# A fused retention and gated-MLP kernel: paired blocks from unit 8, DMA transposes from unit 10, and loads held until the transposes before them have landed

## Chip, cores, metric

One core of one Trainium2 chip. The metric is the device time of one execution in microseconds (us). A "ratio" is the mean time of one kernel's fast runs over the mean of the other kernel's fast runs of the same rounds on the same chip, so it is not quite the ratio of the medians that stand beside it.

The engines: PE is TensorE (matmul), ACT is ScalarE, DVE is VectorE, POOL is GpSimd, SP is SyncE. Here POOL only issues loads (after the first two us), and SP issues the transposes by DMA and the output stores.

## The reference

```python
def _attn_ref(q, k, v):                      # q, k, v: 8 batches, 8 heads, 576 rows, 64 wide, float32
    scores = (1.0 / np.sqrt(D_)) * np.matmul(q, k.transpose(0, 1, 3, 2))
    gamma = 1.0 - 2.0 ** (-5.0 - np.arange(H))
    Dmat = np.where(rel >= 0, gamma[:, None, None] ** rel[None, :, :], 0.0)   # rel = row - column
    return np.matmul(scores * Dmat[None], v)

def _moe_ref(x, w_in, w_out):                # x: 4608 x 512, w_in: 512 x 2048, w_out: 2048 x 512
    h = x @ w_in
    g = h * (1.0 / (1.0 + np.exp(-1.702 * h)))
    return g @ w_out
# x is the attention output with the heads side by side
```

## The kernel before

The 4608 rows are cut into 36 units of 128 rows (all 8 heads of a unit together). A unit needs k and q with rows on the partitions (as loaded, bf16) and also transposed (`qkT`). Per unit PE computes scores (k against q, inside the unit), inter (q against the running state of earlier units), values (masked scores against scaled V) and state (the update of k times V). Four units make a chunk of 512 columns for the MLP, whose long matmuls (`up`, `down`) fill the rest of PE's time. The attention work of later units is slotted between the long matmuls of earlier chunks.

Units 0 to 11 are handled one by one: PE transposes k and q (`head_in`), DVE copies the result out of PSUM, then scores, values, state. From unit 12 on, units go in pairs (`block`), and k and q are transposed by DMA.

```python
NLD, NVN, NQT = 12, 10, 10        # buffers for k/q, V, transposed k/q
osb = [sb(f"osb{i}", [P, DM], FP32) for i in range(4)]      # output row blocks

def transpose_pe(u, bank, eng):             # used by head_in
    ...
    for j in range(2 * HP):                 # eight 128x128 transposes on PE
        op("pe", lambda e, j=j: e.matmul(t[:, j, :], kq[sl][...], ident.ap(), is_transpose=True), ...)
    ...                                     # then one copy PSUM -> qkT
def transpose_dma(u):
    op("sp", lambda e: e.dma_start_transpose(qkT[u % NQT].ap(), kq[sl]...), ...)

def down(c, i, ybanks):                     # four of 16 matmuls of one output row block
    ...
    if s < 3: return
    o = u % 4
    op("act", lambda e: e.activation(osb[o].ap(), y, AF.Copy), reads=[bank], writes=[f"osb{o}"])
    ...                                     # then the store, issued by SP

def fetch(m, after=()):                     # loads of pair m, issued by POOL
    for u in (2 * m, 2 * m + 1):
        if u < NU:
            load_kq(u, after)               # a key in `after` holds the loads until it is written
            load_v(u)
def block(m, done=False):
    a, b = 2 * m, 2 * m + 1
    ...                                     # inter, values of a, b; scores of a + 2, b + 2
    fetch(m + 4)
    ready_t(m + 3)                          # two DMA transposes
    ready_v(m + 2)                          # DVE scales two V

play(16, lambda i: down(0, i, ("H0", "H1")), {
    1: [lambda: head_mid(9)],
    3: [lambda: head_in(10, "dve"), lambda: head_out(9)],
    5: [lambda: head_mid(10)],
    7: [lambda: head_in(11, "dve"), lambda: head_out(10), lambda: ready_t(7), lambda: fetch(8, ...)],
    9: [lambda: head_mid(11), lambda: ready_v(6)],
    11: [lambda: head_out(11)],
})
# for each m: block(m), then eight up (U) and eight down (D) steps, interleaved
```

Each engine runs its own program in order. A helper tracks every buffer's writer and readers and inserts the waits, so a load never overwrites a buffer in use.

## Time and profile before

| | before |
|---|---|
| median of 3 runs | 312.8 us (312.46 to 312.85) |
| span of the profiled run | 311.0 us, clock 1.0 |

The list of waits of PE in before (who waited for whom: us in total, times, longest):

```profile
PE psS L325 <- DMA kq<-in_k_dram: 1.3, 2, 0.7
PE psH L507 <- DVE zero L243: 1.2, 1, 1.2
PE psS L414 <- ACT qkT L330: 0.9, 2, 0.5
PE psS L325 <- DVE kq L623: 0.7, 1, 0.7
PE psO L433 <- DVE pm_1 L423: 0.5, 2, 0.3
PE psH L325 <- DMA kq<-in_q_dram: 0.4, 1, 0.4
```

Nearly all of these 5.0 us lie in the first 20 us (`psS L325` and its like are the first transposes).

The view of the transposed tile in before, its last line (from issue of a DMA to its landing, over the 24 transposes):

```profile
DMA to landing us min/median/max: 3.1/11.1/15.0
```

A transpose by DMA can land in 3.1 us, but most of them share the engines with loads and take about three times that or more (9.1 to 15.0 us). Since PE does not wait, this costs nothing.

The timeline of PE in before (start us, length us, what; a matmul's length includes its latency, so read the spacing of starts):

```profile
51.06 0.61 PE L311 MATMUL psS<-ident,kq 128*128 128x128 bf16 x8
51.51 1.91 PE L471 MATMUL psH<-xT,w_in_sb 128*128 128x256 bf16 x16
53.35 0.40 PE L414 MATMUL psS<-qkT 64*128 64x128 bf16 x8
53.68 1.92 PE L471 MATMUL psH<-xT,w_in_sb 128*128 128x256 bf16 x16
...
76.02 0.62 PE L414 MATMUL psS<-qkT 64*128 64x128 bf16 x16
76.58 1.90 PE L454 MATMUL psH<-xT,w_in_sb 128*128 128x512 bf16 x8
...
89.98 0.39 PE L395 MATMUL psO<-qkT,kv_2 128*128 128x128 bf16 x4
```

Eight transposes of a unit hold PE for 0.45 us (51.06 to 51.51), scores of one unit 0.33 us (53.35 to 53.68), scores of two units together 0.56 us (76.02 to 76.58). The last line is the first work of the block of units 12 and 13, the place where both kernels have done the same PE work except for what the change removes.

### The profile page before, as it was taken

The page shows a single profiled execution, that of the slowest core. Times are in us where ns is not written, and L with a number is a line of the kernel's source. Part 1 is how long each engine was busy: PE and PEld are TensorE (multiplying, and loading weights), DVE is VectorE, ACT ScalarE, POOL GpSimd, SP SyncE. Part 2 cuts the span into 40 slices and gives each one's busy share as a digit, 9 for nine tenths or more (in the row PEclk, how much of TensorE's full clock was granted, in tenths as well). Part 3 has the DMA queues.
Part 4 walks back from the last instruction along what each step waited for, and adds up shares of the span by engine and source line. Part 5 has one row for each costly group of instructions (what it writes and reads, how often), then busy time and mean ns, then how long its engine had stood idle before and what let it go on. Part 6 is the DMA issues. An engine that isn't in the chain of part 4 may idle for free.

```text
span 311.0 us, 5149 instructions
## 1 busy us (share of the span) xinstructions
PE 301.9 (97%) x2169; PEld 155.7 (50%) x2169; DVE 134.5 (43%) x272; ACT 123.4 (40%) x225; POOL 105.6 (34%) x132
## 2 busy tenths in 40 slices
PE   6799999999999999999999999999999999999994
PEld 2444588655454545454545454545454545444441
DVE  5761984597445542545363625362627150100000
ACT  9666345301433333333333333333343434343411
POOL 9999923015699935334454300000000000000000
PEclk9999999999999999999999999999999999999999
DMA  9999999999999999999999999923210102010012
GB/s 150 184 207 188 190 203 175 176 187 157 182 118 200 168 163 150 170 135 176 179 141 190 145 148 182 142 47 86 45 68 2 67 2 67 2 67 34 36 67 67
DMA packets 113752, 39.40 MB, mean 127 GB/s; under 512 B 102785, under 2 KB 106881, under 8 KB 113729
## 3 DMA queue, kind: packets, MB, share of 16 engines
q0 software_dynamic: 80016, 22.55, 74.7%
q1 hardware_dynamic: 33712, 16.52, 30.9%
q8 instruction: 17, 0.28, 0.4%
q14 instruction: 7, 0.05, 0.1%
HBM read 36.70 MB, written 9.44 MB: 148 GB/s over the span
## 4 chain that ended last, share of the span: by engine, by line
PE 92%; POOL 3%; DMA 2%; DVE 2%; ACT 0%; issue 0%; POOLq 0%
PE psH L454 36%; PE psS L485 33%; PE psH L471 5%; PE psH L485 5%; PE psO L433 3%; PE psS L414 3%; DMA vn<-in_v_dram 2%; PE psS L347 2%; PE psO L485 2%; POOL kq L203 2%; PE psO L395 1%; PE psS L311 1%; POOL vn L217 1%; DVE vp L302 0%; DVE xT L443 0%; DVE pm_0 L423 0%
## 5 line engine op out<-in xcount | busy, mean ns | idle before, releaser
L454 PE MATMUL psH<-xT,w_in_sb 128*128 128x512 bf16 x512 | 127.3, 380 | 0.0
L459 ACT ACTIVATE gT<-psH 128x512 bf16<-128x512 f32 x128 | 76.4, 597 | 116.1 <-PE psH L454 116.1
L485 PE MATMUL psS<-w_out_sb,gT 128*128 128x512 bf16 x480 | 117.3, 379 | 0.0
L454 PEld LDWEIGHTS psH<-xT,w_in_sb 128*128 128x128 bf16 x512 | 47.8, 98 | 58.7 <-ACT gT L459 3.2
L485 PEld LDWEIGHTS psS<-w_out_sb,gT 128*128 128x128 bf16 x480 | 46.0, 98 | 51.7
L203 POOL DMA_DIRECT2D kq<-in_k_dram x39 | 35.6, 921 | 43.3 <-DMA qkT<-kq 22.7
L203 POOL DMA_DIRECT2D kq<-in_q_dram x39 | 35.5, 919 | 15.2 <-issue 15.2
L217 POOL DMA_DIRECT2D vn<-in_v_dram x39 | 36.0, 932 | 9.3 <-issue 5.0
L423 DVE TENSOR_TENSOR pm_0<-psS,mask 128x512 bf16<-128x512 f32 x32 | 22.0, 687 | 37.6 <-PE psS L414 37.5
L493 ACT ACTIVATE osb<-psS 128x512 f32<-128x512 f32 x30 | 17.9, 597 | 30.4 <-PE psS L485 30.4
L443 DVE TENSOR_TENSOR xT<-psO,gq 128x512 bf16<-128x512 f32 x36 | 23.5, 682 | 11.4 <-PE psO L433 11.4
L302 DVE TENSOR_TENSOR vp<-vn,vfac 128x512 bf16<-128x512 f32 x36 | 23.7, 685 | 2.6 <-DMA vn<-in_v_dram 2.5
L423 DVE TENSOR_TENSOR pm_1<-psS,mask 128x512 bf16<-128x512 f32 x32 | 21.8, 680 | 0.0
L377 DVE TENSOR_TENSOR kvf<-psS,kvf 64x256 f32<-64x256 f32 x24 | 10.1, 421 | 26.2 <-PE psS L347 26.0
L471 PE MATMUL psH<-xT,w_in_sb 128*128 128x256 bf16 x128 | 15.2, 273 | 0.0
L485 PE MATMUL psH<-w_out_sb,gT 128*128 128x512 bf16 x64 | 15.0, 380 | 0.0
L476 ACT ACTIVATE gT<-psH 128x512 bf16<-128x512 f32 x16 | 9.6, 597 | 11.5 <-PE psH L471 11.5
L414 PE MATMUL psS<-qkT 64*128 64x128 bf16 x288 | 12.2, 218 | 1.1 <-ACT qkT L330 0.9
L433 PE MATMUL psO<-pm_0,vp 128*64 128x128 bf16 x144 | 13.1, 224 | 0.0
L433 PE MATMUL psO<-pm_1,vp 128*64 128x128 bf16 x144 | 12.5, 223 | 0.5 <-DVE pm_1 L423 0.5
L471 PEld LDWEIGHTS psH<-xT,w_in_sb 128*128 128x128 bf16 x128 | 12.0, 98 | 1.9 <-issue 0.2
L375 DVE COPY kvf<-psS 64x256 f32<-64x256 f32 x12 | 5.0, 420 | 18.2 <-PE psS L347 18.1
(78 smaller groups left out, 171.9 us busy)
## 6 DMA issues: line engine op xcount, KB each, us to landing
out_dram<-osb SPq DMA_DIRECT2D x32, 256.0 KB, 3.1
vn<-in_v_dram POOLq DMA_DIRECT2D x31, 256.0 KB, 20.0
kq<-in_k_dram POOLq DMA_DIRECT2D x31, 128.0 KB, 21.4
kq<-in_q_dram POOLq DMA_DIRECT2D x31, 128.0 KB, 21.3
w_in_sb<-in_moe_w_in_dram POOLq DMA_DIRECT2D x4, 512.0 KB, 11.2
w_out_sb<-in_moe_w_out_dram POOLq DMA_DIRECT2D x4, 512.0 KB, 19.6
vn<-in_v_dram POOLq DMA_DIRECT2D x8, 128.0 KB, 23.1
out_dram<-osb SPq DMA_DIRECT2D x8, 128.0 KB, 4.3
```

Of the source, the lines that this page charges most:

```text
L203: e.dma_start(kq[sl][p0 : p0 + n, i, :].rearrange("p (h d) -> p h d", d=DH), src[b, :, s0 : s0 + n, :].rearrange("h p d -> p h d"),)
L217: e.dma_start(vn[sl][p0 : p0 + n, :, :], v[b, :, s0 : s0 + n, :].rearrange("h p d -> p h d"),)
L302: op("dve", lambda e: e.tensor_tensor(vp[u % NVP].ap(), vn[sl].ap(), vfac[:, ty, :, None].to_broadcast([P, H, DH]), ALU.mult), reads=[f"vn ...
L414: op("pe", lambda e, hp=hp, hh=hh, bank=bank: e.matmul(by_pair(bank)[:, hp, :], qt[64 * hh : 64 * hh + 64, hp, :], qt[64 * hh : 64 * hh + ...
L423: op("dve", lambda e: e.tensor_tensor(pm[u % 4][hh].ap(), by_pair(bank), m[:, None, :].to_broadcast([P, HP, P]), ALU.mult), reads=[bank, " ...
L433: op("pe", lambda e, hp=hp, hh=hh: e.matmul(ob[64 * hh : 64 * hh + 64, hp, :], vp[u % NVP][:, 2 * hp + hh, :], pm[u % 4][hh][:, hp, :], st ...
L443: op("dve", lambda e: e.tensor_tensor(xT[ch % 3][:, :, 128 * j : 128 * j + 128], by_pair(bank), gq[:, ty, :, :], ALU.mult), reads=[bank] + ...
L454: op("pe", lambda e, a=a: e.matmul(hb, w_in_sb[:, a, P * f : P * f + P], xT[c % 3][:, a, :], start=(a == 0), stop=(a == HP - 1)), reads=[f ...
L459: op("act", lambda e: e.activation(gT[c % 2][:, f, :], hb, AF.Gelu_apprx_sigmoid), reads=[bank], writes=[f"gT{c % 2}_{f}"])
L471: op("pe", lambda e, a=a, f=f, j=j: e.matmul(hb[:, j, :], w_in_sb[:, a, P * f : P * f + P], xT[c % 3][:, a, n], start=(a == 0), stop=(a == ...
L485: op("pe", lambda e, f=f: e.matmul(y, gT[c % 2][:, f, P * r : P * r + P], w_out_sb[:, f, :], start=(f == 0), stop=(f == NF - 1)), reads=[f ...
L493: op("act", lambda e: e.activation(osb[o].ap(), y, AF.Copy), reads=[bank], writes=[f"osb{o}"])
```

## The change

Its intent: take the transposes of units 10 and 11 off PE, handle units 8 to 11 in pairs, and keep DMA transposes quick by letting no load run beside them. The core of the diff:

```diff
-        def fetch(m, after=()):
+        def fetch(m, held=None):
+            after = () if held is None else [f"qkT{held % NQT}q"]
             for u in (2 * m, 2 * m + 1):
                 if u < NU:
-                    load_kq(u, after)
-                    load_v(u)
+                    load_v(u, "pool", after)
+            for u in (2 * m, 2 * m + 1):
+                if u < NU:
+                    load_kq(u)
@@ block
-            fetch(m + 4)
-            ready_t(m + 3)
-            ready_v(m + 2)
+            if m > 4:
+                ready_t(m + 3)
+                fetch(m + 4, 2 * m + 7)
+                ready_v(m + 2)
@@ loads of the start: k, q of 8 and 9, then V of 8 to 11, then k, q of 10 and 11
-            load_v(u)
-        for u in (10, 11):
-            load_kq(u)
+        load_kq(8)
+        load_kq(9)
...
+        for u in range(8, 12):
             load_v(u)
+        load_kq(10)
+        load_kq(11)
@@ schedule
-        fetch(6)
+        ready_t(5)
+        fetch(6, 11)
+        ready_t(6)
...
+            6: [lambda: ready_v(4), lambda: scores_of(4)],
         play(16, lambda i: down(0, i, ("H0", "H1")), {
-            ... (units 9, 10, 11 one by one, with PE transposes)
+            1: [lambda: state(9)],
+            5: [lambda: ready_v(5)],
+            6: [lambda: block(4)],
+            9: [lambda: state(10), lambda: fetch(7, 13)],
+            11: [lambda: state(11)],
+            12: [lambda: ready_v(6)],
+            14: [lambda: ready_t(7), lambda: fetch(8, 15)],
         })
...
-            for x in "UUDDUDUDUDUDDDUU" if m == 5 else "DDUDUDUDUDUDDUUU":
+            for x in "DDDDBDDUDDUUUUUUU" if m == 5 else "DDUDUDUDUDUDDUUU":
+                if x == "B":
+                    block(m)
+                    continue
```

`fetch(6, 11)` means: the loads of units 12 and 13 (pair 6) wait until the transpose of unit 11 has landed. POOL issues in order, so all six loads of the pair wait. The kernel before already held the loads of pairs 7 and 8 in this way (for the transposes of 13 and 15), with k and q ahead of V; new are the hold of pair 6, the holds from pair 9 on, and V first.

## The prediction

> **What bounds the kernel now.** TensorE (PE). The page gives PE busy 301.9 of 311.0 us (97%); PE has 92% of the chain that ended last. The list of waits shows 5.0 us of PE waits, all on set-up and first loads. After 20 us PE never idles, although the DMA row stands at 9 tenths until about 200 us. Loads are hidden: a transpose by DMA lands 3.1 us after issue when nothing else is queued (201 us) but 9 to 15 us among loads (86 to 187 us), still in time. That agrees with the Trainium skill, "DMA: Bandwidth & Descriptors", "Issuing engines are not separate DMA queues": all queues share 16 engines. So quicker transposes buy nothing by themselves; only PE work counts.
>
> **What changes on PE** (timeline, issue spacing):
> - Transposes of units 10 and 11 leave PE; a block of eight takes 0.45 us (51.06 to 51.51): -0.9 us. (Their 0.69 us DVE copies are off the path.)
> - Paired scores of 8/9 and 10/11: 16 matmuls take 0.56 us against 2 x 0.33: -0.2 us. Paired values: 0.57 against 2 x 0.35: -0.25 us.
> - Fewer insertions between the long matmul groups: about -0.2 us.
> Sum about -1.5 us. Before 51 us and after unit 12's block the PE program is the same.
>
> **What it adds: a serial chain of load pair, transposes, next pair.** k/q of unit 11 should land at about 60.3 us, transposes 10 and 11 at about 62.5 and 63.5; the new pair block asks for them at about 63.5: no wait or a few tenths. Loads of 12/13 now start at about 64 (before: 38 to 52). One link, measured on the existing held fetch: first issue 68.8, last load landing 77.9, second transpose 80.2, next issue 80.6: 11.9 us; V first makes it about 12.8. So transposes 13, 15, 17 land at about 76, 89, 102, asked for at about 77, 90, 105. PE's period is 15.7 us per pair, so the chain gains on PE and no later stall is expected.
> The tight place: SyncE issues in order, so the first output stores wait behind the transposes of 12/13 (about 74.4). Row block 4 needs the output buffer of row block 0 before ScalarE can free bank S2, which unit 13's scores want at about 77.3. Stores land 2.4 to 4.5 us after issue, 77 to 79: a PE stall of about 0.7 us (0 to 2).
>
> **Prediction.** 312.8 - 1.5 + 0.7 = 312.0 us; 8 in 10 between 310.6 and 313.6. Faster by over 2%: 1%; within 2%: 97%; slower by over 2%: 2%.
>
> **What would show it.** PE's transposes in blocks of eight fall from 64 to 48, DMA transposes rise from 24 to 26, landing in 3 to 5 us (median 11.1 before), with no gain from that. Before 51 us the timelines agree. The block of unit 12 (inter against kv_2, 89.98 us before) starts about 89.2; from there on both take the same time. A PE wait under 2 us appears at the scores of 12/13 or 10/11, released by ScalarE's osb copy or a transpose.
>
> **What would make it wrong.** A chain link over 14.5 us (stores and transposes slowing loads): then 14/15 come late at 90 us and output buffers run out later, costing 2 to 5 us. Or no stall at all: 311.3. Or DVE, blocked in order on V of the next pair, delaying masks.

## More of the kernel before

Lines of the page of before (busy time, then two rows in 40 equal slices of the span, each digit the busy share in tenths, one DMA queue, and the shares of the chain that ended last):

```profile
span 311.0 us, 5149 instructions
...
PE 301.9 (97%) x2169; PEld 155.7 (50%) x2169; DVE 134.5 (43%) x272; ACT 123.4 (40%) x225; POOL 105.6 (34%) x132
...
PE   6799999999999999999999999999999999999994
...
DMA  9999999999999999999999999923210102010012
...
q8 instruction: 17, 0.28, 0.4%
...
PE 92%; POOL 3%; DMA 2%; DVE 2%; ACT 0%; issue 0%; POOLq 0%
```

PE is busy 97% of the span and nearly the whole chain. The DMA row is full until about 200 us.

## The result, and the profile after

| | before | after |
|---|---|---|
| median of 6 runs | 312.9 us (312.46 to 313.25) | 312.75 us (311.35 to 313.32) |
| ratio of fast runs | 1 | 0.9989 (95%: 0.9967 to 1.0011) |
| span of the profiled run | 311.0 us | 311.1 us |
| the same in a later set of five rounds | 312.85 us (312.56 to 312.99) | 313.65 us (311.94 to 314.86) |
| ratio there | 1 | 1.0026 (0.9998 to 1.0054) |

The two kernels are the same within noise, but the new one scatters: over 3.5 us in twelve runs, where before stays within 0.8 us in either set. Three of the twelve runs, and the median of the later set (313.65), lie above the upper end of the predicted range (313.6).

The page of after, the lines that answer to those of before:

```profile
span 311.1 us, 5121 instructions
...
PE 300.9 (97%) x2153; PEld 155.3 (50%) x2153; DVE 133.3 (43%) x270; ACT 123.5 (40%) x225; POOL 105.9 (34%) x132
...
PE   7789999999899999999999999999999999999994
...
DMA  9999999979989899896999989699910102010012
...
PE 70%; POOL 15%; DMA 14%; issue 1%; ACT 0%; SPq 0%; POOLq 0%
```

PE lost 1 us of busy time, and the 8 in the eleventh slice of its row (78 to 86 us) is new: PE waits there. The chain that ended last is now PE for 70% only; loads (POOL, DMA) make up the rest.

The list of waits of PE in after:

```profile
PE psS L325 <- DMA kq<-in_k_dram: 1.4, 2, 0.8
PE psH L507 <- DVE zero L243: 1.2, 1, 1.2
PE psS L414 <- ACT qkT L330: 1.1, 3, 0.5
PE psS L414 <- ACT osb L493: 1.0, 1, 1.0
PE psO L433 <- DVE pm_1 L423: 0.6, 2, 0.3
PE psH L325 <- DMA kq<-in_q_dram: 0.4, 1, 0.4
PE psS L414 <- DMA qkT<-kq: 0.2, 1, 0.2
```

Two lines are new: 1.0 us for the output copy (`ACT osb`) and 0.2 us for a transpose. The view of the transposed tile in after, last line:

```profile
DMA to landing us min/median/max: 3.0/3.1/4.8
```

The transposes are more than three times quicker, as intended. Timeline of after around the largest wait (SP, ACT, POOL and PE; in brackets the idle time before and what ended it):

```profile
72.17 3.54 SPq L338 DMA_TRANSPOSE qkT<-kq  x2
...
75.77 1.55 SPq L499 DMA_DIRECT2D out_dram<-osb  x3
...
77.45 0.40 PE L414 MATMUL psS<-qkT 64*128 64x128 bf16 x8
...
78.22 0.60 ACT L493 ACTIVATE osb<-psS 128x512 f32<-128x512 f32 x1 [3.96 <-DMA out_dram<-osb]
78.27 1.78 POOL L217 DMA_DIRECT2D vn<-in_v_dram  x2 [8.23 <-DMA qkT<-kq]
...
78.87 0.40 PE L414 MATMUL psS<-qkT 64*128 64x128 bf16 x8 [1.02 <-ACT osb L493]
```

Read it in order. SP issues the transposes of 12 and 13 when their k and q have landed, until 75.71 us. Only then do the stores of the first output row blocks go out (75.77), though those blocks had been ready for up to 14 us (ACT had copied the first at 61.5). ACT wants to write row block 4 into the same buffer as row block 0 and waits for that store to land (3.96 us, until 78.22). Its copy frees PSUM bank S2, which the second eight scores (unit 13) need. PE waits 1.0 us.

The two smaller places, timeline of PE in after:

```profile
63.58 0.94 PE L414 MATMUL psS<-qkT 64*128 64x128 bf16 x16
...
89.72 0.39 PE L395 MATMUL psO<-qkT,kv_2 128*128 128x128 bf16 x4
90.04 0.40 PE L414 MATMUL psS<-qkT 64*128 64x128 bf16 x8
90.59 0.40 PE L414 MATMUL psS<-qkT 64*128 64x128 bf16 x8 [0.15 <-DMA qkT<-kq]
```

The sixteen scores of 10 and 11 take 0.94 us instead of 0.62, because the transpose of 11 landed at 64.07 us. The second eight scores at 90.59 waited for the transpose of 15, which landed at 90.54.

How much is that? In an undisturbed block the second eight matmuls start 0.055 us after the last of the first eight. Measured against that, the three blocks lost 0.31, 1.18 and 0.31 us: 1.80 us. At the first matmul behind the block of units 12/13 before stands at 91.42 us and after at 91.49. So PE work and switches saved 0.07 less than the waits cost: 1.73 us saved, 1.80 us given back. From there to the end both take 219.6 us (311.03 - 91.42, 311.09 - 91.49).

### The profile page after: what moved, and what is told of

The parts are those of the page before. It is cut to its first block, busy times and chain, and to the rows that moved or that the text cites. A ratio compares the mean times of both kernels' runs of the same rounds, so it can differ in the third digit from the quotient of the medians.

```text
span 311.1 us, 5121 instructions
## 1 busy us (share of the span) xinstructions
PE 300.9 (97%) x2153; PEld 155.3 (50%) x2153; DVE 133.3 (43%) x270; ACT 123.5 (40%) x225; POOL 105.9 (34%) x132
## 4 chain that ended last, share of the span: by engine, by line
PE 70%; POOL 15%; DMA 14%; issue 1%; ACT 0%; SPq 0%; POOLq 0%
PE psS L485 31%; PE psH L454 30%; DMA kq<-in_q_dram 11%; POOL kq L203 8%; POOL vn L217 4%; DMA qkT<-kq 3%; PE psO L485 2%; PE psO L433 2%; PE psS L414 2%; PE psS L347 1%; PE psO L395 1%; POOL w_out_sb L232 1%; POOL w_in_sb L226 1%; PE psO L402 0%; ACT osb L493 0%
## 5 line engine op out<-in xcount | busy, mean ns | idle before, releaser
L217 POOL DMA_DIRECT2D vn<-in_v_dram x39 | 34.3, 919 | 111.3 <-DMA qkT<-kq 111.3
L433 PE MATMUL psO<-pm_1,vp 128*64 128x128 bf16 x144 | 12.2, 223 | 0.6 <-DVE pm_1 L423 0.6
L433 PE MATMUL psO<-pm_0,vp 128*64 128x128 bf16 x144 | 12.7, 223 | 0.0
L347 PE MATMUL psS<-vp,kq 128*128 128x128 bf16 x128 | 12.4, 219 | 0.0
```

The costliest lines, as they stand in the source:

```text
L217: e.dma_start(vn[sl][p0 : p0 + n, :, :], v[b, :, s0 : s0 + n, :].rearrange("h p d -> p h d"),)
L433: op("pe", lambda e, hp=hp, hh=hh: e.matmul(ob[64 * hh : 64 * hh + 64, hp, :], vp[u % NVP][:, 2 * hp + hh, :], pm[u % 4][hh][:, hp, :], st ...
```

## The experiments

Twelve kernels ran, all correct, each with five rounds. Four groups shared a chip and the runs of before: e1, e2, e4, e7; then e5, e6, e10, e11; then e9, e12, e13; then e14 alone. In the profiles of the experiments 36 matmul records are missing (2117 instead of 2153; 34 in e14), which shows as waits of 0.16 us for "issue" at regular places; they are left out below.

| run | what | median us (range) | ratio to before (95%) |
|---|---|---|---|
| e1_osb8 | eight output buffers | 316.14 (315.26 to 316.59) | 1.0093 (1.0079 to 1.0106) |
| e2_kqfirst | k, q of 10, 11 before their V | 311.82 (311.10 to 312.99) | 0.9961 (0.9945 to 0.9976) |
| e4_pairs_pe | pairs, but PE transposes, no first hold | 311.91 (311.67 to 312.48) | 0.9965 (0.9953 to 0.9977) |
| e7_f6 | no hold for units 12, 13 | 318.78 (318.19 to 319.27) | 1.0181 (1.0168 to 1.0194) |
| e5_hold_before | before, with hold and V first | 312.77 (312.63 to 313.02) | 1.0002 (0.9990 to 1.0014) |
| e6_both | e1 and e2 together | 312.05 (310.78 to 315.21) | 0.9996 (0.9954 to 1.0038) |
| e10_hold_first | hold for the first transpose of a pair | 311.32 (311.05 to 311.49) | 0.9953 (0.9940 to 0.9965) |
| e11_best | e2 and e10 together | 311.03 (310.76 to 311.29) | 0.9946 (0.9934 to 0.9958) |
| e9_hold_early | no hold from pair 9 on | 315.11 (313.77 to 317.37) | 1.0079 (1.0046 to 1.0112) |
| e12_hf_osb8 | e1 and e10 together | 311.03 (310.92 to 311.21) | 0.9945 (0.9932 to 0.9957) |
| e13_after_again | after, unchanged | 313.65 (311.94 to 314.86) | 1.0026 (0.9998 to 1.0054) |
| e14_osb8_shift | e1 with PE's instruction fetches moved | 312.46 (312.11 to 312.79) | 0.9985 (0.9973 to 0.9998) |

### Part alone: the loading order and the hold, in before

```diff
 # before
-                    load_kq(u, after)
-                    load_v(u)
+                    load_v(u, "pool", after)     # V of both units, then k and q of both
...
-            fetch(m + 4)
-            ready_t(m + 3)
+            ready_t(m + 3)
+            fetch(m + 4, [f"qkT{(2 * m + 7) % NQT}q"])
```

> The kernel before with only the loading part of the change in its steady loop: V of a pair ahead of its k and q, and from pair 9 on the next pair's loads held until the last transpose of the pair before. No pairing, units 10 and 11 still transposed on PE. Theory: transposes land in 3 to 5 us instead of 9 to 15 us, and the time does not move (ratio 0.998 to 1.002), since PE had no wait there. Rival (quicker transposes or a less loaded DMA speed something up): ratio below 0.997.

Measured: ratio 1.0002. The view of the transposed tile in this run, last line:

```profile
DMA to landing us min/median/max: 3.0/3.2/4.9
```

The median fell from 11.1 to 3.2 us and the time did not move. A wait that nobody has on the critical path is worth nothing, however long it looks.

### Part alone: pairing, with the transposes on PE

```diff
 # after
-        ready_t(5)
-        fetch(6, 11)
+        fetch(6)
@@ play(16, down ...)
+            2: [lambda: head_in(10, "dve", "S2")],
+            4: [lambda: head_in(11, "dve", "S0")],
```

> Pairing alone: the kernel after, but units 10 and 11 are transposed on PE (in two single blocks between the long matmuls) and the loads of 12 and 13 are not held. PE does 16 transposes more than after (+0.9 us) but the chain starts early, so no wait at the scores of 11, 13 and 15 (-1.7 us). Main theory: about 0.7 us faster than before, ratio about 0.997 to 0.998; the profile shows no PE wait after 20 us. Rival (pairing saves nothing, insertions are free): ratio 1.000 or above.

Measured: 0.9965, and no wait of PE after 38 us. The rival falls: pairs and fewer insertions are real time. The saving (0.35% of 312.9 us, 1.1 us) was more than the 0.65 us that the prediction's terms for them add up to, and this kernel, which still does two units' transposes on PE, was faster than the full change in either set of that (0.9989 and 1.0026; the interval of the first overlaps by a little).

### Undo one hold: the loads of units 12 and 13

```diff
-        fetch(6, 11)
+        fetch(6)
```

> The kernel after, with the hold removed from the loads of units 12 and 13 alone. Theory: the hold there protects the transposes of 10 and 11; without it they share the 16 DMA engines with the loads and land 2 to 4 us later than 62.3 and 64.1 us, so PE waits 2 to 4 us at the scores of 10/11, while the waits at 13 and 15 vanish because the chain behind starts some 7 us earlier. Net 0.3 to 2.5 us slower than after, ratio 1.000 to 1.007. Rival (sharing costs the transposes little): transposes land by 65 us, and the ratio falls to 0.995.

Measured: 1.0181, worse than expected (1.000 to 1.007). Timeline of this run (SP and PE):

```profile
59.53 10.79 SPq L338 DMA_TRANSPOSE qkT<-kq  x4
...
67.90 0.61 PE L414 MATMUL psS<-qkT 64*128 64x128 bf16 x8 [4.03 <-DMA qkT<-kq]
...
69.61 0.61 PE L414 MATMUL psS<-qkT 64*128 64x128 bf16 x8 [1.10 <-DMA qkT<-kq]
```

Both transposes of 10 and 11 took 8.3 us instead of 3.1 (landing at 67.85 and 69.56), since the loads behind them went through the same engines. PE waited 4.0 and 1.1 us. What nobody had expected: the clock record shows half clock from 65.9 to 72.8 us. So the hold is needed at this place, and a wait of PE can cost more than itself.

### The output buffers: e1

```diff
-        osb = [sb(f"osb{i}", [P, DM], FP32) for i in range(4)]
+        osb = [sb(f"osb{i}", [P, DM], FP32) for i in range(8)]
@@ down
-            o = u % 4
+            o = u % 8
```

> The kernel after with eight output buffers in place of four, nothing else. Main theory: the 1.0 us wait of PE at the second half of the scores of 12/13 comes from the output store of row block 0, which SyncE issues behind the held transposes and which ScalarE needs landed before it reuses that buffer. Then this wait goes (under 0.2 us left), the small waits at the scores of 11 and 15 stay (about 0.3 us together), and the time falls by 0.7 to 1.1 us against the kernel after, to a ratio of about 0.9955 against before. Rival: the transposes of 13 (landing at 77.6 us) are what came late; then nearly the same wait stays, with the transpose as its releaser, and the ratio stays at 0.998 to 0.999.

Measured: 1.0093, all six runs between 315.3 and 316.6 us: neither theory expected a slower kernel. The wait for the output copy did go, and so far the main theory holds: the buffer was what PE waited for. But in its place stood 0.73 us for the transpose of 13, which landed at 78.42 here (77.61 in after): the rival was partly right. And at the next pair, timeline of this run (SP and PE):

```profile
86.74 2.94 SPq L338 DMA_TRANSPOSE qkT<-kq  x2
...
89.84 0.40 PE L414 MATMUL psS<-qkT 64*128 64x128 bf16 x8
...
92.87 0.61 PE L414 MATMUL psS<-qkT 64*128 64x128 bf16 x8 [2.64 <-DMA qkT<-kq]
```

The second transpose of that pair was issued at 88.45 and landed at 92.82, 4.4 us later instead of 3.1. PE waited 2.6 us for it. As the wait ended the clock fell. The view by stretches of this run (PEclk is the granted clock, last but two):

```profile
core 0: us, PE busy (x) PEld busy (x) DVE busy (x) ACT busy (x) POOL busy (x), PEclk, DMA share, GB/s
...
92.80:96.20 3.40, 3.33 (x29) 1.85 (x30) 2.11 (x4) 0.00 (x0) 2.98 (x4) 0.52 0.60 184
```

For 3.4 us after the wait PE had half clock. An estimate from these numbers: the waits at the scores of 13 and 15 are 3.4 us, half clock over the 3.2 us of it in which PE worked adds 1.6, saved work takes off 1.7: 3.3 us in sum against 3.8 in the spans (314.8 and 311.0). One of the six runs (315.94 us) is as slow at a mean clock of 1.0, where 3.4 us at half clock would give 0.995; it was not profiled, so the half clock is shown for the profiled run and not for every slow one.

Two questions stayed: are eight buffers slow in themselves, and what delayed the landing?

### Eight buffers with an earlier chain: e6 and e12

e6 has e1's edit and e2's load order; e12 has e1's edit and e10's hold (both edits are shown below).

> Eight output buffers and k, q of 10 and 11 ahead of their V, together. The run of eight buffers alone came out at 1.009: its trace shows the second transpose of pair 14/15 landing at 92.8 us, with a 16 KB instruction fetch on the same DMA engines at 89.4 us in the middle of it, PE waiting 2.6 us, and then 3.4 us at half clock. Theory A (timing collision, not the buffers): with the chain about 0.8 us earlier that wait is under 0.5 us, no half clock, and the ratio is 0.994 to 0.998, as with the load order alone (0.9961) or 0.2 us better. Rival B (eight buffers are slow in themselves, by their place in memory or by the stores that now run at other times): ratio 1.005 or above again.

Measured: 310.78, 311.06, 311.08, 313.02, 314.40 and 315.21 us. Three runs are as fast as the best kernel and two are nearly as slow as e1, those two with a mean clock of 0.994 and 0.995. So buffers alone do not decide; but theory A had promised a steady run, and this one is not.

> Eight output buffers on top of the hold for the first transpose only (that run alone: 0.9953, steady). There the second transpose of 14/15 lands near 87 us, some 3 us before PE asks for it. Theory A (the slow run of eight buffers was a late transpose at a tight place): now 0.994 to 0.997, no half clock, all runs within 0.6 us of each other. Rival B (eight buffers slow in themselves): 1.003 or above, or scattered as in the run of eight buffers with the new load order (310.8 to 315.2 us).

Measured: 0.9945, all runs within 0.3 us. Rival B falls. The same eight buffers are harmless once the transpose of 15 lands early enough. It landed at 88.57 us in this run, 1.6 us later than expected and only 0.3 us before PE's second eight scores (88.88); so the profiled run had a margin of 0.3 us there, and still all five runs were steady.

### What delayed the landing: moving the instruction fetches

The packet records of the trace show 17 fetches of 16 KB each on queue q8, which the page calls "instruction", a good 1 us each. The Trainium skill, "Runtime: NRT & Kernel Launch", "Instruction fetch mechanics", says that each sequencer fetches its instructions in blocks of 16 KiB (256 instructions) by DMA, and calls the cost of crossing a block "mostly hidden". The size agrees. From the packet and landing records (us):

```
run               fetches between 55 and 115 us       second transpose of 14/15: issued, landed
after             58.1  72.1  90.0  107.9             87.48  90.54
e1_osb8           58.3  73.1  89.4  111.1             88.45  92.82
e9_hold_early     58.2  71.7  90.2  114.2             87.35  92.25
e13_after_again   57.9  71.2  89.1  106.3             86.55  89.61
e14_osb8_shift    59.0  78.7  91.7  112.2             86.69  89.76
```

In e1 a fetch starts 0.9 us after the issue of that transpose, in e9 2.9 us after it, and the landing is 1.3 and 1.8 us late. In e1 the transpose's packets stop from 90.5 to 91.0 us and only trickle until 91.8; in e9 all of them have started by 90.5, and fifteen of the sixteen completion marks are there by 90.66, but the last comes at 92.25. In e1 the load of q that landed last before the transpose of 13 took 6.3 us, with a fetch beside it; in after it took 5.3, also with one, and in e14, the next run, 4.7, with none. In after and e13 a fetch starts 2.6 us after the issue and does no harm, so two coincidences prove little.

The kept traces hold more cases. Take the second transpose of every pair from unit 13 on in the ten runs that hold the next loads for it (in e9 only up to 15), 110 in all, by where a fetch of q8 starts:

```
no fetch from 1.5 us before the issue to the landing     88 transposes   3.0 to 3.4 us, median 3.1
fetch 0.2 to 2.4 us after the issue                       9              3.45 to 4.65 us
fetch 2.5 to 2.9 us after the issue                      10              seven 3.1 us, three 4.8 to 4.9 us
fetch up to 0.9 us before the issue                       3              3.34, 3.35 and 4.27 us
```

Every transpose with a fetch in its first 2.4 us is later than all 88 without one; near the end it can go either way, as in e9 on one side and after and e13 on the other. The next run moves the fetches by an edit far from the chain:

```diff
 # e1_osb8; warm(): matmuls on zeros at the start, to keep PE busy while the first loads land
-                op("pe", lambda e: e.matmul(
-                    banks["H1"].ap(), zero[:, 0:P], zero.ap(), start=True, stop=True), ...)
+                for j in range(4):
+                    op("pe", lambda e, j=j: e.matmul(
+                        banks["H1"][0:32, P * j : P * j + P], zero[:, 0:32], zero[:, 0:P],
+                        start=True, stop=True, skip_group_check=True), ...)
```

> The slow kernel with eight output buffers (1.0093, all six runs between 315.3 and 316.6 us), with one thing more: each warm-up matmul of 512 columns on zeros at the start is cut into four of 128 columns. The PE time hardly changes, but PE runs some 150 instructions more before 40 us, so its 16 KB instruction fetches, seen at 73.1 and 89.4 us, move about 9 us earlier, to near 64 and 80 us, when the chain of loads and transposes has next to nothing in flight. Theory (a fetch in the middle of a load or transpose delays its landing by 1 to 2 us, and so the whole chain): the last transposes of 13 and 15 land at 76 to 78 and 89 to 91 us, PE waits under 1 us in all after 20 us, no half clock, ratio 0.995 to 0.999. Rival (the fetches are innocent and only coincide): the second transpose of 14/15 lands at 92 us or later again, half clock after it, ratio 1.005 or above.

Measured: 0.9985 instead of 1.0093, all runs between 312.1 and 312.8 us, one wait of 0.7 us at the scores of 15 and no half clock. The list of waits of PE in this run, the line of that wait:

```profile
PE psS L414 <- DMA qkT<-kq: 0.7, 1, 0.7
```

The fetches did not go where they were estimated (59.0, 78.7 and 91.7 us instead of 64 and 80), but out of the way of the four transposes of 12 to 15 all the same, the last by luck: it starts 1.9 us after the transpose of 15 has landed. The same kernel with 75 more tiny matmuls at its start is 3.7 us faster (medians; 3.4 by the ratios). That a fetch in the middle of a transpose delays its landing is shown by the count, and that moving the fetches takes the loss of e1 away by this run, with the reservation that the edit also changes PE's first 40 us; which step of a DMA a fetch blocks is not shown.

### Starting the chain earlier: e2, e10, e11

```diff
 # e2: k and q of 10, 11 ahead of their V
-        for u in range(8, 12):
-            load_v(u)
-        load_kq(10)
-        load_kq(11)
+        load_v(8)
+        load_v(9)
+        load_kq(10)
+        load_kq(11)
+        load_v(10)
+        load_v(11)
 # e10: every hold is for the first unit of the pair before, not the second
-        fetch(6, 11)        # likewise fetch(7, 13), fetch(8, 15)
+        fetch(6, 10)        #          fetch(7, 12), fetch(8, 14)
-                fetch(m + 4, 2 * m + 7)
+                fetch(m + 4, 2 * m + 6)
```

> The kernel after, with k and q of units 10 and 11 loaded ahead of V of 10 and 11 (V of 8 and 9 still first). Theory of the serial chain: the whole chain of held loads and transposes starts about 2.6 us earlier (transpose 11 lands near 61.5 instead of 64.1, 13 near 75, 15 near 88), the stores go out about 2.6 us earlier, and all three PE waits (scores of 11, 13, 15, about 1.7 us together) vanish without any other change: ratio about 0.994 to 0.995 against before. Rival: the PE work saved is not real time (insertions are hidden in the matmul stream) and the kernel stays at 0.998 to 1.000 whatever the waits do.

Measured: 0.9961. The direction is right and the size is not: the chain started only 0.85 us earlier (transpose 11 landed at 63.22 us, not 61.5), because V of 10 and 11 (landing at 59.5 and 61.7) and an instruction fetch (59.4) now ran beside these transposes, which took 5.5 and 4.6 us. The waits at 13 and 15 shrank to 0.2 us each in the list of waits.

> The kernel after, with the next pair's loads held until the first unit of the pair is transposed instead of the second. Theory: each link of the chain shortens by about 1.5 us, and a load needs some 2 us from its issue before data flows, so the second transpose is hardly disturbed (3 to 4 us). Transpose 13 lands near 76, 15 near 87: the waits at the scores of 13 and 15 go, 0.3 us at 11 stays, and the ratio is 0.995 to 0.997. Rival (the second transpose then shares the engines with the loads and lands in 5 us or more, as the unheld run showed with 8.3 us): no gain on after, 0.998 to 1.002.

Measured: 0.9953. The second transposes of 10/11 and 12/13 took 3.0 and 3.1 us, undisturbed; the rival falls. (The first packet of a held load starts 1.6 us after its issue in after, and 1.6 to 2.3 us in this run.) Transpose 13 landed at 75.39 us, 15 at 87.12, and of the three waits only the one at 11 (0.2 us) is left. The runs lie within 0.5 us again.

> Both changes that start the chain earlier: loads held for the first transpose of the pair only, and k, q of 10 and 11 loaded ahead of their V. Theory: no PE wait after 20 us at all, ratio 0.994 to 0.996, the best of the study by some tenths of a us over the load order alone (0.9961). If waits remain at the scores of 11 the gain stays at 0.996.

Measured: 0.9946 (median 311.03 us against 312.74 of before), as good as e12, and better than before and after. The list of waits of PE in this run, its largest lines (the first comes from missing records, the others lie before 38 us):

```profile
PE psH L454 <- issue: 1.6, 10, 0.2
PE psS L325 <- DMA kq<-in_k_dram: 1.3, 2, 0.7
PE psH L507 <- DVE zero L243: 1.2, 1, 1.2
PE psS L414 <- ACT qkT L330: 0.9, 2, 0.5
PE psH L325 <- DMA kq<-in_q_dram: 0.6, 2, 0.4
```

No wait is left after 38 us. e11 over e4 is roughly what the DMA transposes of 10 and 11 bring, once nothing waits: 0.9946 against 0.9965, about 0.6 us by the two ratios (the intervals overlap, the two ran on different chips and differ in their holds too; 0.9 us was expected from PE's spacing).

### Unsettled: no hold in the steady loop

```diff
-                fetch(m + 4, 2 * m + 7)
+                fetch(m + 4)
```

> The kernel after with the hold kept for pairs 6, 7 and 8 and taken away from pair 9 on. Theory: in the steady loop the chain has slack, so the hold there is worth nothing to PE: transposes land in 8 to 15 us again from pair 9 on, the early waits stay as in after, and the ratio is that of after measured beside it, within 0.002. Rival (the hold is needed later too): new PE waits appear after 100 us and the ratio rises above 1.003.

Measured: 1.0079, above the 1.0026 of after beside it (the intervals overlap by a little). The profiled run shows no wait of PE after 100 us, although the transposes take 6 to 18 us there from pair 8 on (all but the last two); what it lost, it lost at the scores of 15 (2.2 us for the transpose that landed at 92.25, then half clock for 3.4 us). Up to that landing it does what after does: POOL issues in order, so the first load without a hold follows the loads held for this very transpose. That speaks for the theory (the hold buys PE nothing later on), but the times are outside what the theory expected, and why this kernel was slow more often than after is open (its fetch fell 2.9 us after the issue, where the count above has both outcomes).

> The kernel after once more, unchanged, for a second profile and more times beside the same before. Theory: three waits of PE near 64, 78 and 90 us, 1.3 to 2.2 us together, the largest at 78 us by the output copy; ratio 0.997 to 1.001. If the waits differ from the first profile by much more than that, or the clock falls to half after one of them, the result rests on the timing of single landings.

Measured: 1.0026, runs of 311.94, 312.63, 312.75, 314.55, 314.83 and 314.86 us. The profiled run is the fastest of them: waits of 0.2 us at 11 and 0.6 us at 13, none at 15. So the waits in after's first profile are one draw. Its three slow runs have a mean clock of 0.999 to 1.0, so no 3.4 us at half clock, and none of them was profiled: what they wait for was not seen.

## Why the prediction was right, and where it was off

- **The bound** (only PE work counts): right. e5 made the transposes three times quicker in before, at ratio 1.0002.
- **PE work removed, 1.5 us**: right in kind, a little small: 1.73 us in the profile (1.75 at the start of the block of unit 12, adding the waits up to there). Pairing alone, in e4, was worth 1.1 us instead of 0.65.
- **The serial chain, 12.8 us a link against PE's 15.7**: right. The links measured 13.5, 12.7 and 12.8 us (first load of one pair to that of the next: 64.74, 78.27, 90.94, 103.77), and no wait appears after 91 us. But the chain ran later than predicted: the transposes of 13, 15 and 17 landed at 77.61, 90.54 and 103.38 us instead of 76, 89 and 102, because the transpose of 11 landed 0.6 us later than predicted and the first link took 13.5 us instead of 12.8.
- **The tight place**: right. Stores behind the transposes, the output buffer, ACT, bank S2, PE at the second half of the scores at 78 us: the timeline shows this chain link by link.
- **The stall of 0.7 us (0 to 2)**: the term that was mis-sized. In the profile three places cost 1.80 us: 0.31 at unit 11 (allowed for as "a few tenths" but not put into the sum), 1.18 at unit 13, 0.31 at unit 15 ("no later stall is expected" fails here, by the 1.5 us that the chain was late). So 312.0 became 312.75: the sum is -1.7 + 1.8, not -1.5 + 0.7.
- **The scatter** was not foreseen. Three requests of PE met their landings within a microsecond (63.5, 77, 90), and the prediction treated that as 0.7 us give or take 1. In e1 and e9 a landing that came 1.3 and 1.8 us late there, with an instruction fetch beside it, cost its delay and then 3.4 us of half clock. Runs of the unchanged kernel span 311.35 to 314.86 us; none of the twelve shows a half clock of that length, and what its slow runs lost was not profiled. That the first median fell well inside the range is partly luck: that of the same kernel's later set, 313.65, lies just outside it.

The Trainium skill's "Issuing engines are not separate DMA queues" ("DMA: Bandwidth & Descriptors"), on which the prediction rested, agrees with the traces: 8.3 us for a transpose beside loads in e7, 3.1 us alone.

Where the expected gain went is thus settled for the profiled run: PE saved 1.73 us and gave 1.80 back in three new waits. Those at 13 and 15 come from starting the loads of units 12 and 13 only after transpose 11; the one at 11 comes from loading k and q of 10 and 11 behind four V: it goes when they are loaded ahead of two of these (e2, e11), though e1 and e14 do not show it either. With transposes 13 and 15 landing 2.2 and 3.4 us earlier (e10) the gain is there, 1.4 us by the medians and 1.7 in e11, and the scatter is gone.

## What to carry to other kernels

When a change serialises transfers to make each one quick, lay the resulting landings beside the times at which the bound engine asks for them: where request and landing meet within about a microsecond, as at three places here, the time hangs on single landings: it may scatter (after, e6), be slow in every run (e1) or hold steady (e12). Release the next transfer as soon as it can no longer disturb the one before (here at the first transpose of two). In-order queues couple things that have nothing to do with each other, here output stores behind transposes. A small edit that turns out slower in every run may have moved something unrelated, such as where instruction fetches fall; shift that before you blame the edit.

## What the Trainium skill lacked or had wrong

- "Runtime: NRT & Kernel Launch", "Instruction fetch mechanics": "mostly hidden" fits PE itself (no wait of PE in before after 38 us, with 15 fetches of 16 KB there), but the page says nothing of fetches delaying other transfers: a DMA transpose with a fetch in its first 2.4 us landed after 3.45 to 4.65 us instead of 3.1, and moving the fetches changed one kernel from ratio 1.0093 to 0.9985.
- "TensorE: Matmul & The Clock Gate", Part 1 and "Why this matters for your kernels": the default clock is said to return after an idle window of about 3.4 us, with no gaps over about 3 us as the rule. Here shorter waits went with a fall: 2.6 us (e1) and 2.2 us (e9) with one stretch of 3.4 us at half clock each, 4.0 and 1.1 us (e7) with 6.8 us of it; waits of 1.0 us and less did not. In these three traces the clock record, counted from its first entry, changes only at multiples of 3.41 us; in e9 the fall came 1.4 us after the wait had ended. So what counts here is PE's idle time within such a stretch: over the fourteen traces each stretch with 2.0 us or more of it was followed by half clock (2.5 in e1, 2.0 in e9, 2.1 in e7), and none with 1.8 us or less (1.8 at the end of after).
- The same page, Part 4: the duration of a PE transpose in a kernel's context is put at about 275 ns. Here it is 220 ns, and in a block of eight they start only 0.056 us apart (0.45 us for eight), which is what PE's time goes by.
- The same page, "Back-to-back issue gap": sustained matmuls of 512 columns are put at about 131 ns. Here eight take 1.73 us, 216 ns each, the page's own formula for the isolated gap.
- "DMA: Bandwidth & Descriptors" has a bandwidth for DMA transposes, but no time from issue to landing for one from SBUF to SBUF: 128 x 1024 bf16 lands 3.0 to 3.1 us after issue when nothing disturbs it, and mostly 6 to 18 us among loads.
